# Filling transfers moved from SyncE's queue to GpSimd's, with new planner constants, in a four-layer attention kernel

## The chip, the core and the metric

The kernel runs on one core of a Trainium2 chip. The time is the device time of one execution in microseconds (us). Engines are named as in the profile: PE (TensorE), ACT (ScalarE), DVE (VectorE), POOL (GpSimd) and SP (SyncE, which only issues DMAs here).

## What is computed

Four layers with residuals: attention A, linear attention B, then A and B again with the same weights. S is 2048, D is 512, and there are 32 heads of 16. In A all heads share one K and V.

```python
def _A_ref(x, wq, wk, wv, wo):
    q = (x @ wq).reshape(B, S, H, Dh).transpose(0, 2, 1, 3)
    k = x @ wk
    v = x @ wv
    scores = jnp.einsum("bhqd,bkd->bhqk", q, k) * (Dh ** -0.5)
    p = _softmax(scores, axis=-1)
    o = jnp.einsum("bhqk,bkd->bhqd", p, v)
    return o.transpose(0, 2, 1, 3).reshape(B, S, H * Dh) @ wo
...
x = x + _A_ref(_layernorm(x), A_wq, A_wk, A_wv, A_wo)
x = x + _B_ref(_layernorm(x), B_wqkv, B_wo)      # phi(q) (phi(k)^T v) / den, then @ wo
x = x + _A_ref(_layernorm(x), A_wq, A_wk, A_wv, A_wo)
x = x + _B_ref(_layernorm(x), B_wqkv, B_wo)
```

## The kernel before

**A planner writes the order.** The kernel is a program that records operations (`op`, with the engine, a duration, what is read and written, and a priority) and plays them through in a model of the engines (`Planner`, L36). Whatever is ready first by the model, and of these the lowest priority number, is next on its engine. The order that comes out is fixed at build time. On the chip every engine goes through its list strictly in order, and waits on semaphores where data or a buffer is not there yet. So durations in the code are plan times: they decide the order, not how long something takes.

**Attention layers (L = 0 and 2, `run_a`, L950).** The 2048 scores blocks of a layer (128 keys by 512 columns, 16 query tiles x 2 parities x 16 key tiles x 4 row groups) are made on PE by L959, three to four row groups at a time. The exponential of a block is taken in one of two ways:

- ACT takes two or three blocks at once (L1139) into a PT buffer, and PE multiplies them with V into the accumulator bank (L1013).
- DVE makes an approximate exponential of one block (L1225): it adds a constant to the scaled scores and reads the int16 bits as a bf16 number. Four blocks make a chunk in an FB buffer of 128x2048. The approximation is smoothed with three more copies of the chunk, each with another constant added to the int16 bits, and weighted copies of V (`VW`). So each DVE block costs PE four multiplications.

A copy is made in one of two ways. DVE makes it with one instruction for the chunk (L1273). Or two DMAs make one of the three: a **filling transfer** (`prime`, L1285, issued at L1297) first writes the constant from a row in DRAM (`shift_row`) into a free FB buffer, and an **addition** (`dma_shift`, L1304, issued at L1306) then adds the finished chunk to that buffer in the DMA engines. Up to NPRE = 2 buffers stand filled ahead (`primed`). `dve_shifts` (L1253) takes the DMA way for a chunk when a filled buffer is there, more than DMIN query segments are left, and the planned end of the DMA backlog (`pl.dmaq`) is less than DQ ahead.

**Queues.** Fillings are issued from SP (hardware queue q1 of the profile), additions from POOL (software queue q0). SP also issues the DMA transposes (`dmat`, L737): 24 of `OT<-Osb` in the epilogues of the attention layers (`epilogue`, L1396), which the product with `wo` on PE (L731) reads, and 36 of `xnT<-xn` (12 at the start, 24 for the tiles of the B layers that are worked on beside the attention). POOL also does two small operations of each layer norm (L813, L815), on which DVE waits at L818. SP and POOL, too, wait in order: a filling at the head of its queue that waits for PE to finish with its buffer holds all that stands behind it.

**Plan times of the DMAs.** An operation with `xfer=(a, b)` is planned to land at `dmaq + b`, where `dmaq` is moved on by `a` after the issue's own duration and `lat` (L191 to L193): one line for fillings and additions together. A filling has 0.54 + 0.2 for the issue and (DPF, DTAIL), an addition has PGEN + 0.3 = 0.95 + 0.3 and (DXF, DTAIL). A transpose has 0.1 and DTL = 4.0, outside of `dmaq`.

**Constants by stage.** The module's constants (L368 to L441) hold until `act_stream` replaces some of them: at L1066 the first attention layer applies `TUNE[0]` at the very start, and at L1069 each attention layer applies its own dictionary. Nothing is reset, so what TUNE[0] sets and TUNE[2] doesn't also holds in layer 2. The other thresholds: CHT, CHE, ENDL (how many blocks ahead DVE may take from), FBO, FBS, FBP (how many FB buffers must stay free for a new chunk, for copies, for a filling), AHEAD, BLS, BLT, BLO, DXB (how much planned work DVE may have in front of it when it is given a block), STICK (whether PE keeps its mode), LAG (how long an engine waits for a more urgent operation).

**B layers (`run_b`, L1461)** have little PE and ACT work, much of it laid beside the attention layers. The change touches nothing there.

Of the kernel before, what the change touches and what calls it, by code (L numbers as in the profile page):

```python
# [8 lines left out]
I16 = mybir.dt.int16  # L9
# [3 lines left out]
PE, AC, DV, PO, SP = "pe", "act", "dve", "pool", "sp"  # L13
ENGS = (PE, AC, DV, PO, SP)

P = 128
# [19 lines left out]
class Planner:  # L36
# [41 lines left out]
    def op(self, opts, reads=(), writes=(), prio=5.0, lat=0.08, dma=False, name="", join=None, mode="full", port=False, after=(), behind=(), xfer=None):  # L78

        o = Op()  # L80
        o.opts, o.prio, o.users, o.done, o.end = opts, prio, [], False, None
        o.eng, o.fn, o.n, o.value, o.sem, o.signal, o.isdma = None, None, None, None, None, False, dma
        o.name = (name, lat)
        o.freed = False
        o.begun = None
        o.cols = 0
        o.mode = mode
        o.port = port
        o.xfer = xfer
        deps = set()  # L90
        for k in reads:
            deps.update(self.ws(k))
        for k in list(writes) + list(after) + list(behind):
            deps.update(self.ws(k))
            deps.update(self.readers.get(k, ()))
        if join is not None:
            deps.update(join.deps)
            deps.discard(join)
        for k in writes:
            if join is not None and join in self.ws(k):  # L100
                self.writer[k] = self.ws(k) + [o]
            else:
                self.writer[k] = [o]
                self.readers[k] = []
        for k in list(reads) + list(after):
            if k not in writes:
                self.readers.setdefault(k, []).append(o)
        o.deps = deps
        o.left = 0
        chain = len(opts) == 1 and PE in opts  # L110
        for d in deps:
            if not (d.done or (chain and d.freed and d.eng == PE)):
                o.left += 1
                d.users.append(o)
        if o.left == 0:
            self._eligible(o)
        return o
# [226 lines left out]
class Seg:  # L344
# [11 lines left out]
    def take(self, js, back=False):  # L356
# [22 lines left out]
LAG = 0.15  # L379
# [16 lines left out]
BLS = 1.4  # L396
BLO = 5.0
DXB = 2.0
BLT = 2.5
# [18 lines left out]
CHB = 4  # L418
FBO = 2
FBS = 4  # L420
AHEAD = 20
CHT = 19
PSH = False
STICK = 1.5
# [4 lines left out]
DMIN = 4  # L429
NPRE = 2  # L430
EVEN = True
CHE = 8
AVOID = True
PGEN = 0.95
DPF = 2.2
DXF = 2.8
DTAIL = 1.6
DQ = 4.0
FBP = 4
TUNE = {0: {"DXF": 4.5, "DTAIL": 2.0, "CHT": 26, "FBO": 1, "FBS": 3, "AHEAD": 8, "BLS": 2.3, "BLT": 2.8, "FBP": 4, "DQ": 6.0, "DMIN": 4, "LAG": 0.25, "BLO": 3.5, "STICK": 2.5, "DXB": 2.0},  # L440
        2: {"CHE": 8, "DMIN": 3, "NPRE": 2, "BLS": 1.7}}  # L441


def bass_interleave_layers__grouped_kv_mqa__linear_attn_block__prompt_kernel(
# [12 lines left out]
    op = pl.op  # L457
# [39 lines left out]
    FB = sb("FB", [P, NFB, CHB * 512], BF16)  # L497
# [23 lines left out]
    pts, fbs = {}, {}  # L521
# [28 lines left out]
    def once(tag, keys):  # L550
        if tag in seen:
            return ()
        seen.add(tag)
        return keys

    def guest(L, kind, i, h=None):
        return once((L, kind, i, h), home[kind, i]) if (kind, i) in home else ()
# [131 lines left out]
    cst = nc.dram_tensor("shift_row", (1, CHB * 512), I16, kind="Internal").ap()  # L689

    def fb_keys(i):
        return [("FB", i, h) for h in range(CHB)]
# [46 lines left out]
    def until(*keys):  # L739
        for k in keys:  # L740
            yield ("ops", pl.ws(k))
# [208 lines left out]
    def run_a(L):  # L950
# [23 lines left out]
        def spend(h, o):  # L974
            h[0] -= 1
            if o not in h[1]:
                h[1].append(o)
            if h[0] == 0:
                pl.give_after(h[2], h[3], h[1])
# [85 lines left out]
        def act_stream():  # L1065
            if L == 0:  # L1066
                globals().update(TUNE[0])
            yield ("flag", ("K", L, 0))
            globals().update(TUNE[L])  # L1069
            if L:  # L1070
# [214 lines left out]
        def prime():  # L1285
            yield ("flag", ("K", L, T - 1))
            if L == 0:
                row = FB[0:1, NFB - 1, :].bitcast(I16)
                op({DV: (0.6, lambda e: e.memset(row, DSH * 128 // NSH))}, writes=fb_keys(NFB - 1), prio=1.0)
                op({SP: (0.54, lambda e: e.dma_start(cst, row))}, reads=fb_keys(NFB - 1), writes=["cst"], prio=1.0, lat=2.5, dma=True)  # L1290
            yield from until("cst")
            while state["si"] < len(segs) - DMIN:
                if len(primed) >= NPRE or len(fb_pool.free) <= FBP or fb_pool.wait:
                    yield ("sleep", 0.2)
                    continue
                g_ = yield ("acq", fb_pool, 9.0)
                o = op({SP: (0.54, lambda e, g_=g_: e.dma_start(fbs[g_].bitcast(I16), cst.to_broadcast([P, CHB * 512])))}, reads=["cst"], writes=fb_keys(g_), prio=9.0,  # L1297
                       lat=0.2, dma=True, behind=guest(L, "FB", g_), xfer=(DPF, DTAIL))
                primed.append((g_, o))
            while primed:  # L1300
                g_, o = primed.pop()
                pl.give_after(fb_pool, g_, [o])

        def dma_shift(blk, f_, hold, g_, o):  # L1304
            pl.stat["dma"] += 1
            o = op({PO: (PGEN, lambda e: e.dma_start(fbs[g_].bitcast(I16), fbs[f_].bitcast(I16), accum_op=ALU.add))}, reads=fb_keys(f_), writes=fb_keys(g_), prio=0.0, lat=0.3,  # L1306
                   dma=True, xfer=(DXF, DTAIL))
            spend(hold, o)
# [32 lines left out]

        pl.process(spare())
        pl.process(prime())
        for i in pairs:
            pl.process(spare_sacc(i))
# [564 lines left out]
```

## Time and profile before

| | |
|---|---|
| median of 3 runs | 1512.31 us (1508.14 to 1513.63) |
| the profiled execution | 1501.68 us |
| its span, first to last instruction | 1499.9 us |
| attention layers, steady parts | 10 to 620 us and 850 to 1410 us |
| B layers alone | about 700 to 850 us, and from 1410 us |
| additions (L1306) | 163, on POOL |
| fillings (L1297) | 167, on SP |

The profile gives for each group of instructions the busy time, the mean duration of one, and the idle time of the engine before them with what ended it. "Us to landing" of a DMA is from the start of its issuing instruction to the last step of its semaphore. A wait is put down to the semaphore that came last. SP is shown as SPq since it is never busy, and a DMA's own time shows only in the shares of the queues.

### The profile page before, as it was taken

Reading aid. Unit: us, or ns where it says so; the run is one execution under the profiler, and the core shown is the slowest. Engines: PE = TensorE matmul, PEld = TensorE weight load, DVE = VectorE, ACT = ScalarE, POOL = GpSimd, SP = SyncE. Lnnn points to the kernel's source line nnn. Section 1 sums busy time; section 2 is a strip of 40 time slices with the busy share of each in tenths; the row PEclk is TensorE's granted clock in tenths of the full one; section 3 lists DMA queues with packets and bytes.
Section 4 is the critical chain, followed back from the end, with each engine's and each line's share of the span. In section 5 each row is a group of like instructions: output and inputs, shape, how many; then the busy total and the mean of one; then the engine's idle time right before and its main releaser. Section 6 shows DMA issues by size and latency. Waiting matters only on the chain.

```text
span 1499.9 us, 37236 instructions
## 1 busy us (share of the span) xinstructions
PE 1403.9 (94%) x14791; PEld 509.3 (34%) x14906; DVE 1416.7 (94%) x2615; ACT 1444.2 (96%) x1511; POOL 245.8 (16%) x353
## 2 busy tenths in 40 slices
PE   7999999999989899999999999998999999999998
PEld 4333333233323233233644332332333333333335
DVE  7999999999989999999876999998999999999996
ACT  8999999999989999999799999998999999999996
POOL 5111121111111112000111111121211111111001
PEclk9999999999999999999999999999999999999999
DMA  4766767666676667311000276766767666766101
GB/s 118 208 150 148 181 144 180 168 148 158 150 159 155 150 154 174 85 29 51 9 2 2 58 173 144 161 150 148 164 161 170 170 156 147 173 158 161 24 16 57
DMA packets 89021, 191.72 MB, mean 128 GB/s; under 512 B 39441, under 2 KB 46097, under 8 KB 88850
## 3 DMA queue, kind: packets, MB, share of 16 engines
q0 software_dynamic: 23472, 85.47, 30.5%
q1 hardware_dynamic: 65378, 103.87, 23.3%
q8 instruction: 120, 1.97, 0.5%
q14 instruction: 51, 0.42, 0.1%
HBM read 93.88 MB, written 2.10 MB: 64 GB/s over the span
## 4 chain that ended last, share of the span: by engine, by line
PE 20%; ACT 15%; DVE 13%; issue 5%; DMA 3%; POOL 1%; ACTq 0%; POOLq 0%
ACT PT L1139 9%; PE ps L1013 6%; PE ps L959 6%; ACT xnT L1139 4%; DVE FB L1225 4%; PE ps L731 3%; DVE FB L1273 3%; PE ps L1058 2%; PE ps L892 1%; DMA FB<-FB 1%; DVE OBB L1225 1%; DVE sacc L1225 1%; DMA OBB<-FB 1%; DMA xn<-FB 1%; ACT phE L1467 1%
## 5 line engine op out<-in xcount | busy, mean ns | idle before, releaser
L1139 ACT ACTIVATE PT<-ps 128x1024 bf16<-128x1024 f32 (+1 forms) x946 | 1005.8, 1169 | 12.9 <-PE ps L959 11.4
L959 PE MATMUL ps<-QT,KM 32*128 32x512 bf16 x4096 | 537.5, 385 | 44.1 <-ACT PT L1139 19.0
L1225 DVE TENSOR_SCALAR FB<-ps 128x512 int16<-128x512 f32 x828 | 545.7, 683 | 18.2 <-PE ps L959 16.8
L1013 PE MATMUL ps<-FB,VW 128*32 128x512 bf16 x3247 | 452.5, 385 | 7.3 <-DVE sacc L1359 1.7
L1013 PE MATMUL ps<-PT,V 128*32 128x512 bf16 x2097 | 380.9, 388 | 13.8 <-ACT PT L1139 5.5
L959 PEld LDWEIGHTS ps<-QT,KM 32*128 32x128 bf16 x4096 | 134.6, 91 | 425.3 <-ACT PT L1139 194.2
L1139 ACT ACTIVATE xnT<-ps 128x1024 bf16<-128x1024 f32 (+1 forms) x238 | 261.9, 1152 | 7.2 <-PE ps L959 6.9
L1273 DVE TENSOR_SCALAR FB<-FB 128x2048 int16<-128x2048 int16 x365 | 244.9, 681 | 0.2
L1139 ACT ACTIVATE OBB<-ps 128x1024 bf16<-128x1024 f32 (+1 forms) x166 | 182.2, 1144 | 3.2 <-PE ps L959 3.2
L1013 PEld LDWEIGHTS ps<-FB,VW 128*32 128x32 bf16 x3247 | 109.9, 94 | 128.2 <-issue 75.8
L1058 PE MATMUL ps<-QT,V 128*32 128x512 bf16 (+6 forms) x623 | 150.3, 318 | 1.3 <-DVE FB L1225 0.7
L1306 POOL DMA_DIRECT2D FB<-FB x77 | 77.0, 1001 | 426.1 <-DVE FB L1225 314.3
L1013 PEld LDWEIGHTS ps<-PT,V 128*32 128x32 bf16 x2097 | 91.9, 93 | 100.6 <-issue 48.2
L1013 PE MATMUL ps<-xnT,V 128*32 128x512 bf16 x524 | 121.2, 388 | 1.3 <-ACT xnT L1139 0.6
L1013 PE MATMUL ps<-OBB,V 128*32 128x512 bf16 x361 | 83.5, 390 | 2.7 <-ACT PT L1139 1.4
L813 POOL TENSOR_SCALAR ve<-mv 128x1 f32<-128x1 f32 x64 | 30.7, 482 | 316.2 <-DVE mv L812 314.7
L1058 PEld LDWEIGHTS ps<-QT,V 128*32 128x32 bf16 x623 | 48.5, 95 | 69.0 <-issue 47.1
L731 PE MATMUL ps<-wqkv,xnT 128*128 128x512 bf16 (+1 forms) x204 | 64.9, 370 | 3.9 <-issue 2.1
L1013 PE MATMUL ps<-wq,VW 128*32 128x512 bf16 x256 | 63.2, 386 | 0.3 <-issue 0.3
L1013 PE MATMUL ps<-xn,VW 128*32 128x512 bf16 x275 | 62.8, 384 | 0.1
L1013 PE MATMUL ps<-OBB,VW 128*32 128x512 bf16 x237 | 57.7, 388 | 1.2 <-DVE sacc L1359 0.8
L1225 DVE TENSOR_SCALAR xn<-ps 128x512 int16<-128x512 f32 x81 | 53.7, 683 | 1.2 <-PE ps L959 1.0
(210 smaller groups left out, 1650.7 us busy)
## 6 DMA issues: line engine op xcount, KB each, us to landing
FB<-shift_row SPq DMA_DIRECT2D x115, 512.0 KB, 4.8
FB<-FB POOLq DMA_DIRECT2D x77, 512.0 KB, 5.7
sacc<-shift_row SPq DMA_DIRECT2D x15, 512.0 KB, 4.5
wo<-shift_row SPq DMA_DIRECT2D x15, 512.0 KB, 5.7
sacc<-FB POOLq DMA_DIRECT2D x12, 512.0 KB, 5.1
FB<-xn POOLq DMA_DIRECT2D x12, 512.0 KB, 5.4
wo<-FB POOLq DMA_DIRECT2D x11, 512.0 KB, 5.4
OBB<-shift_row SPq DMA_DIRECT2D x10, 512.0 KB, 6.2
```

What stands on the lines that cost most here:

```text
L731: return e.matmul(dst, lhsT=l, rhs=r, start=(k == 0), stop=(k == len(pairs) - 1))
L813: op({PO: (0.1, lambda e: e.tensor_scalar(out=ve[:, t:t + 1], in0=mv[:, t, 1:2], scalar1=1e-5, scalar2=None, op0=ALU.add))}, reads=[("mv", ...
L892: ins = e.matmul(dst[:, g * P:(g + 1) * P], lhsT=lhs(g, k), rhs=rhs(k), start=(k == 0), stop=(k == FT - 1))
L959: return e.matmul(bank(b), lhsT=KM[r, sg.par, kt * P:(kt + 1) * P], rhs=QT[r, sg.t, :], start=True, stop=True)
L1013: ins = e.matmul(ps[32 * j:32 * j + 32, ACC * 512:(ACC + 1) * 512], lhsT=V[:, kt, :] if w is None else VW[:, kt, w, :], rhs=ap, start=(k = ...
L1058: o = op({PE: (n / 2400.0, lambda e: e.matmul(ps[32 * j:32 * j + 32, b * 512:b * 512 + n], lhsT=V0[:], rhs=QT[:, sg.t, 0:n], start=st, sto ...
L1139: ex = op({AC: (0.051 + 0.4267 * n, lambda e, n=n, s_=s_, p_=p_: e.activation(pts[p_][:, 0:n * 512], ps[:, s_ * 512:(s_ + n) * 512], ACTF. ...
L1225: o = op({DV: (0.602, lambda e: e.tensor_scalar(out=dst.bitcast(I16), in0=bank(b), scalar1=VB, scalar2=VLO, op0=ALU.add, op1=ALU.max))}, w ...
L1273: o = op({en: (du, lambda e, w=w, g_=g_: e.tensor_scalar(out=fbs[g_][:, 0:n].bitcast(I16), in0=fbs[f_][:, 0:n].bitcast(I16), scalar1=float ...
L1306: o = op({PO: (PGEN, lambda e: e.dma_start(fbs[g_].bitcast(I16), fbs[f_].bitcast(I16), accum_op=ALU.add))}, reads=fb_keys(f_), writes=fb_k ...
L1467: op({AC: (0.07 + n / 1200.0, lambda e: e.activation(phE[:, i, 0:n], bank(b, n), ACTF.Exp))}, reads=[B_(b)], writes=[("phE", i)], prio=pr ...
```

## The change

Three things change. The filling is issued by POOL instead of SP, with the plan time of an addition's issue (PGEN = 0.95) and 0.3 after it. The module's DPF, DXF and DTAIL are 2.0, 3.4 and 2.0. And both TUNE dictionaries are new; TUNE[0] no longer sets DXF, DTAIL, FBO, AHEAD, BLT, DQ or STICK.

```diff
 PGEN = 0.95
-DPF = 2.2
-DXF = 2.8
-DTAIL = 1.6
+DPF = 2.0
+DXF = 3.4
+DTAIL = 2.0
 DQ = 4.0
 FBP = 4
-TUNE = {0: {"DXF": 4.5, "DTAIL": 2.0, "CHT": 26, "FBO": 1, "FBS": 3, "AHEAD": 8, "BLS": 2.3, "BLT": 2.8, "FBP": 4, "DQ": 6.0, "DMIN": 4, "LAG": 0.25, "BLO": 3.5, "STICK": 2.5, "DXB": 2.0},
-        2: {"CHE": 8, "DMIN": 3, "NPRE": 2, "BLS": 1.7}}
+TUNE = {0: {"CHT": 26, "FBS": 3, "BLS": 1.2, "BLO": 5.0, "DXB": 0.8, "FBP": 3, "DMIN": 3, "LAG": 0.25},
+        2: {"FBO": 3, "FBP": 6, "DQ": 6.0, "NPRE": 2, "LAG": 0.2, "BLS": 1.7, "BLO": 7.0, "CHT": 26, "DMIN": 2}}
...
-                o = op({SP: (0.54, lambda e, g_=g_: e.dma_start(fbs[g_].bitcast(I16), cst.to_broadcast([P, CHB * 512])))}, reads=["cst"], writes=fb_keys(g_), prio=9.0,
-                       lat=0.2, dma=True, behind=guest(L, "FB", g_), xfer=(DPF, DTAIL))
+                o = op({PO: (PGEN, lambda e, g_=g_: e.dma_start(fbs[g_].bitcast(I16), cst.to_broadcast([P, CHB * 512])))}, reads=["cst"], writes=fb_keys(g_), prio=9.0,
+                       lat=0.3, dma=True, behind=guest(L, "FB", g_), xfer=(DPF, DTAIL))
```

Since the order is planned, it changes on every engine. The built program of the changed kernel has 193 additions and 197 fillings, all of them on POOL, and on SP only loads, transposes and stores are left.

## The prediction

> **What bounds the kernel now.** I read the page's first part, then the busy time of five stretches: the two attention layers (their steady parts, 10 to 620 us and 850 to 1410 us), and three windows of 50 us in them with lost time (columns after the length: PE, weight loads, DVE, ACT, POOL; clock; DMA share).
>
> ```profile
> span 1499.9 us, 37236 instructions
> PE 1403.9 (94%) x14791; PEld 509.3 (34%) x14906; DVE 1416.7 (94%) x2615; ACT 1444.2 (96%) x1511; POOL 245.8 (16%) x353
> 10.00:620.00 610.00, 574.17 (x6014) 191.90 (x6059) 593.83 (x1076) 599.65 (x612) 112.94 (x148) 0.99 0.67 158
> 850.00:1410.00 560.00, 525.33 (x5579) 176.44 (x5615) 548.89 (x986) 548.85 (x563) 94.32 (x106) 0.99 0.66 152
> 400.00:450.00 50.00, 43.58 (x444) 13.82 (x446) 44.18 (x78) 44.16 (x45) 7.11 (x9) 0.93 0.65 140
> 500.00:550.00 50.00, 45.16 (x493) 14.70 (x494) 47.87 (x86) 47.63 (x50) 8.72 (x10) 1.00 0.69 154
> 1000.00:1050.00 50.00, 44.68 (x478) 16.12 (x481) 44.41 (x81) 44.57 (x48) 8.46 (x8) 0.93 0.59 137
> ```
>
> In the attention layers ACT is busy for 599.65 of 610 and 548.85 of 560 us, with DVE as full beside it. ACT bounds the kernel, and only 10.35 + 11.15 = 21.5 us of its idle time there can be won. Of that, 5.84 + 2.37 + 5.43 us lie in the three windows. What ended the waits in them (first row: 417 to 425 us, then 498 to 512, 1208 to 1222, 1004 to 1020; us in total, times, longest), and who waited for the DMA transposes of L737 in the whole span:
>
> ```profile
> ACT OBB L1139 <- PE ps L959: 3.0, 1, 3.0
> ...
> ACT PT L1139 <- PE ps L959: 2.3, 1, 2.3
> ...
> ACT PT L1139 <- PE ps L959: 1.2, 1, 1.2
> ...
> ACT xnT L1139 <- PE ps L959: 4.6, 2, 4.0
> PE ps L1013 <- DMA FB<-FB: 3.6, 1, 3.6
> ...
>   PE ps L959: 5.8, 2
> ...
>   PE ps L731: 2.2, 1
> DMA to landing us min/median/max: 2.4/2.7/8.9
> ```
>
> The lost time has two sources. One addition (L1306) held PE for 3.6 us and ACT for 4.6. Three late transposes held PE for 5.8 + 2.2 = 8.0 us, and ACT for 3.0 + 2.3 + 1.2 = 6.5. The change can act through these two kinds of lateness, or through the work itself.
>
> **The change, part by part.** *What is really planned.* The diff raises the module's DXF from 2.8 to 3.4, but that value was not in force: TUNE[0] was applied from the first instant (L1066) and never taken back, so every addition of before was planned with DXF 4.5, DTAIL 2.0. The new TUNE has neither, so an addition's plan goes from 0.95 + 0.3 + 4.5 + 2.0 = 7.75 us to 0.95 + 0.3 + 3.4 + 2.0 = 6.65: shorter, not longer. A fill's goes from 0.54 + 0.2 + 2.2 + 2.0 = 4.94 to 5.25. A transpose keeps 0.1 + 4.0. What they took (last column, us to landing):
>
> ```profile
> FB<-shift_row SPq DMA_DIRECT2D x115, 512.0 KB, 4.8
> FB<-FB POOLq DMA_DIRECT2D x77, 512.0 KB, 5.7
> ```
>
> The median addition (5.7) still lies inside 6.65 and the median fill inside 5.25.
>
> *Work.* Counted in the built order, DVE blocks (L1225) go from 1114 to 1116, shift copies on DVE (L1273) from 665 to 644 whole ones and from 15 to 0 short ones, additions from 163 to 193, fills from 167 on SP to 197 on POOL. ACT's exponentials (L1139) go from 1068 of 1024 columns and 282 of 1536 to 1100 and 260; ACT also loses six copies (3 va, 3 xnT) and gains three.
>
> ```profile
> L1273 DVE TENSOR_SCALAR FB<-FB 128x2048 int16<-128x2048 int16 x365 | 244.9, 681 | 0.2
> L1139 ACT ACTIVATE PT<-ps 128x1024 bf16<-128x1024 f32 x741 | 744.9, 1076 | 11.7 <-PE ps L959 10.3 <-PE ps L1013 0.4
> L1139 ACT ACTIVATE PT<-ps 128x1536 bf16<-128x1536 f32 x205 | 303.5, 1505 | 1.2 <-PE ps L959 1.1
> ```
>
> DVE: 21 x 244.9/365 = 14.1 us less, the 15 short ones between 0 and 15 x 0.67 = 10 (I take 5), two blocks more at about the same 0.67: -18 us. ACT: 32 x 744.9/741 - 22 x 303.5/205 = -0.4 us; three copies of 512 columns, each no more than the 1.0 us of 1024: **-2 us** in all, the range -0.4 to -3.4. So DVE is relieved but ACT, which bounds, is not: the 18 us are cover, not time.
>
> *Issue on POOL.* Each of the 197 fills now costs POOL an issue like an addition's:
>
> ```profile
> L1306 POOL DMA_DIRECT2D FB<-FB x77: 852/871/2431, 48.2 to 1384.9; - x77
> SPq L1297 <- PE ps L1013: 192.9, 72, 12.8
> DVE xn L818 <- POOL rs L815: 10.8, 18, 1.2
> ```
>
> With 30 more additions that is 227 x 0.87 to 227 x 2.43, or 200 to 550 us, on an engine busy for 245.8 of 1499.9: hidden. What queues behind a fill counts more: on SP fills waited for PE to free their buffer (72 times for L1013 alone), and on POOL the next addition and the layer norm's L813 and L815 stand behind that wait. DVE waits 10.8 us for L815 now; twice that is the price if it grows with the issues, and the 18 us above cover it. I take 0, with 0 to +10 as the range.
>
> The Trainium skill, page "DMA: Bandwidth & Descriptors", section "SWDGE vs HWDGE vs iDMA", speaks against this part: GpSimd writes its descriptors into SBUF, from which DVE's two-port modes lock it out, while DMAs issued from SP are immune. The median of 871 ns beside a minimum of 852 shows little of that here; at the maximum for every fill the sum would still stay on POOL.
>
> *Additions.* One late addition cost ACT 4.6 us. The chain's longest DMA pieces, and the two queues in 1006.5 to 1010 us, while the first of them was under way:
>
> ```profile
> 959.30 9.01 DMA xn<-FB
> 1005.68 11.40 DMA FB<-FB
> 1098.92 9.09 DMA OBB<-FB
> ...
> 1006.58 0.32 SPq L1297 DMA_DIRECT2D sacc<-shift_row  x1
> 1007.44 0.32 SPq L1297 DMA_DIRECT2D OBB<-shift_row  x1
> 1008.53 0.32 SPq L1297 DMA_DIRECT2D FB<-shift_row  x1
> ...
> q1 hardware_dynamic: 142, 0.54, 64.2%
> ```
>
> Fills issued after the addition overtook it on the other queue: in that window only q1 moved. In one queue, behind it, they can't. I take **-5 us**; the range goes to +15, if 193 additions planned 1.1 us shorter come late one time in twenty, by 1.5 us each.
>
> *Transposes.* They now have SP's queue to themselves, but everything else shares q0. The two queues while an addition (issued just before, landing at 507.8) and the transpose of 501.67 were both under way, 503 to 505.5 us, and once the addition had drained, 506 to 507.5 (packets, MB, share of 16 engines); then the whole run:
>
> ```profile
> q0 software_dynamic: 134, 0.48, 101.6%
> q1 hardware_dynamic: 76, 0.02, 5.9%
> OT<-Osb SPq DMA_TRANSPOSE x1, 6.6
> ...
> q1 hardware_dynamic: 398, 0.14, 58.1%
> q0 software_dynamic: 20, 0.02, 16.2%
> ...
> 501.67 1.45 SPq L737 DMA_TRANSPOSE OT<-Osb  x1
> 503.23 1.11 SPq L1297 DMA_DIRECT2D wq<-shift_row  x1
> ...
> q0 software_dynamic: 23472, 85.47, 30.5%
> q1 hardware_dynamic: 65378, 103.87, 23.3%
> ```
>
> While q0 has packets the transpose gets 76 small ones in 2.5 us, against 398 in 1.5 us afterwards: it advances by small packets between large ones and in effect lands when q0 runs dry (6.6 us; planned 4.1). Two fills issued after it (the first at 503.23) did not hold it, for they stood behind it in its own queue. After the change they would be in q0 and pass it. Load of q0 over the 1170 us of the two stretches: before, 0.305 x 1499.9 = 457 us of all engines (2.81 an addition), 39%. After, 193 x 2.81 = 542 and 197 fills at no more than 0.233 x 1499.9 / 167 = 2.09 us, 412: 954 us, 81%.
>
> The Trainium skill, same page, section "Queues, rings and completion order", says that each engine round-robins between queue rows a packet at a time, a packet being typically 9 to 17 descriptors. The turns agree with the rows; the size doesn't, for 76 transpose records against 134 of q0 is less than one to a turn. By the page's size a transpose would need few turns, and the rival "faster" below would hold.
>
> Price: if lateness grows with q0's share (39 to 81%), the 8.0 us of PE waits become 17; if with share over free share (0.64 to 4.3), 54. Between ends so far apart I take 28, near the 17, because the plan lets an addition start only under a bounded backlog: 20 us more on PE. ACT lost 6.5 for 8.0, but the 400 us window lost 5.84 for one stall of 3.0, since the clock fell to 0.93; I count one for one: **+20 us**, range -6.5 (all transposes on time) to +46.
>
> *Sum:* 20 - 5 - 2 + 0 = +13 us. The profiled execution took 1501.68 us, its span 1499.9 and 1.8 around it; with the change 1514.7. It lies 10.6 us below the median of the three runs shown (1512.31), and I take the same distance afterwards: **1525 us**, +0.9%.
>
> **The rivals.**
> *Faster.* One queue in order makes landings regular, and a transpose is hardly held. Place: L737 and L1306. For it: the three additions of 9 to 11 us and the overtaking. Against it: 76 against 398 packets. It decides if transposes still land within 4.1 us under q0's load. Price -6.5 - 5 - 2 = -13.5: 1512.31 - 13.5 = **1499**, and down to 1491 with all 21.5 us won.
> *No change.* q0's backlog stays short, since fills are issued when buffers come free and not at random; transposes lose only what additions win, +7: **1512**.
> *Slower still.* The 1.1 us taken from the plan of additions, and fills holding POOL's queue while they wait for PE, make additions late too: 46 + 15 + 10 - 2 = +69 at the far end of all, half of it more likely: **1545**.
> *It doesn't do what it says.* The longer plan is none, as shown; that is already in the sum.
>
> **How the numbers follow.** Forecast 0.38, slower still 0.14, no change 0.26, faster 0.22. A difference within 0.5% (7.6 us) is about what a measurement of this kernel can't tell from none. Forecast and "slower still" both give slower: 0.52; same 0.26; faster 0.22. The range leaves out a tenth on either side: the lower half of "faster" (below 1497) and the upper half of "slower still" (above 1550). The forecast's own range is 1515 to 1538.
>
> **What would show it.** Right: PE waits for `OT<-Osb` and `xnT<-xn` grow from 8.0 us to 20 or more and the transposes' median landing rises above 4 us; more windows with a clock under 1.00; the chain has fewer additions over 8 us; ACT's busy time stays within 3 us of 1444, DVE's falls by about 18. Wrong: transposes land at 2.7 as before, or PE waits mostly for additions, or ACT's busy time moves by over 5 us, which would mean that the plan and not the queues decides.

## The result and the profile after

The changed kernel takes 1549.94 us (median of 4 runs, 1543.25 to 1554.53), the kernel before, run beside it, 1512.97 (4 runs, 1508.14 to 1514.02). The ratio is **1.0247, 95% interval 1.0204 to 1.0291**: slower by 37 us. The forecast was 1525, +0.9%. The profiled execution of after took 1550.07 us.

The page of after, its first part, then queues, then DMA issues (last column: us to landing):

```profile
span 1548.3 us, 37399 instructions
...
PE 1423.3 (92%) x14803; PEld 510.5 (33%) x14915; DVE 1410.5 (91%) x2584; ACT 1447.5 (93%) x1518; POOL 394.9 (26%) x580
...
q0 software_dynamic: 56160, 204.50, 58.4%
q1 hardware_dynamic: 41330, 16.30, 5.4%
...
FB<-shift_row POOLq DMA_DIRECT2D x142, 512.0 KB, 7.0
FB<-FB POOLq DMA_DIRECT2D x91, 512.0 KB, 5.7
```

ACT does almost the same work (1444.2 us before, 1447.5 now), but its idle time rose from 1499.9 - 1444.2 = 55.7 to 1548.3 - 1447.5 = 100.8 us. So the span's 48.4 us are 45.1 of idle ACT and 3.3 of work. The additions land as before (5.7), but a filling now needs 7.0 us instead of 4.8. Who waited for the transposes of L737 in the kernel after:

```profile
  PE ps L731: 21.2, 7
  PE ps L959: 11.9, 4
...
  PE ps L892: 9.8, 3
...
DMA to landing us min/median/max: 2.4/4.8/13.7
```

PE lost 21.2 + 11.9 + 9.8 = **42.9 us** to late transposes, against 8.0 before. The median landing went from 2.7 to 4.8 us, past the planned 4.1, and the longest to 13.7. For the additions of L1306 in the kernel after, the same view has:

```profile
  PE ps L1013: 1.9, 3
...
DMA to landing us min/median/max: 4.5/5.7/12.9
```

In the kernel before it has:

```profile
  PE ps L1013: 6.5, 6
```

So the additions did win something, and the transposes lost far more. In the chain of waits of after the longest DMA pieces (start, us) are now mostly transposes, where before three additions stood:

```profile
1009.24 12.85 DMA OT<-Osb
...
1127.03 10.37 DMA xnT<-xn
1158.25 13.69 DMA OT<-Osb
...
1277.06 10.62 DMA FB<-wo
1362.35 9.78 DMA xnT<-xn
1461.41 9.00 DMA OBB<-FB
```

One of them from close by, in the timeline of after (start, us, engine; in brackets the idle time before and what ended it):

```profile
1123.18 1.16 POOL L1306 DMA_DIRECT2D FB<-FB  x1 [3.90 <-DVE FB L1225]
...
1124.29 1.20 POOL L1297 DMA_DIRECT2D wq<-shift_row  x1
...
1125.58 2.63 POOL L1297 DMA_DIRECT2D FB<-shift_row  x3
1127.03 1.20 SPq L737 DMA_TRANSPOSE xnT<-xn  x1
1131.13 0.90 POOL L1306 DMA_DIRECT2D wq<-wo  x1 [2.92 <-DMA wq<-shift_row]
1133.07 0.87 POOL L1306 DMA_DIRECT2D FB<-FB  x1 [1.04 <-DMA FB<-shift_row]
...
1137.44 0.61 PE L892 MATMUL ps<-xnT,wqkv 128*128 128x128 bf16 x4 [5.98 <-DMA xnT<-xn]
```

POOL waited for DVE and then issued an addition and four fillings in a burst. The transpose of 1127.03 met them, two more additions were issued while it was under way, and it landed after 10.37 us. PE, in its fixed order, stood for 5.98 us. What that cost (windows of after; ACT's busy time is the fourth pair, the clock the third number from the end):

```profile
10.00:640.00 630.00, 575.76 (x6005) 191.86 (x6050) 589.92 (x1061) 599.05 (x606) 174.61 (x246) 0.98 0.73 162
870.00:1460.00 590.00, 541.93 (x5597) 176.94 (x5630) 548.04 (x973) 552.92 (x577) 172.86 (x222) 0.96 0.82 180
...
1125.00:1131.00 6.00, 5.77 (x76) 1.61 (x68) 6.00 (x11) 6.00 (x8) 3.22 (x5) 1.00 0.91 263
1131.00:1137.00 6.00, 0.39 (x3) 0.10 (x3) 2.00 (x4) 1.86 (x3) 1.77 (x2) 0.72 1.04 213
1137.00:1143.00 6.00, 5.56 (x39) 2.24 (x39) 2.44 (x4) 3.03 (x4) 0.00 (x0) 0.50 0.78 154
1143.00:1149.00 6.00, 6.00 (x39) 1.94 (x34) 4.68 (x9) 4.15 (x5) 0.00 (x0) 0.64 0.01 3
1149.00:1155.00 6.00, 5.84 (x62) 1.81 (x59) 5.70 (x12) 6.00 (x7) 1.50 (x2) 1.00 0.71 154
```

ACT lost 4.14 + 2.97 + 1.85 = 9.0 us for a PE wait of 6.0. PE was busy again from 1137.44 on, but at half clock, and it didn't feed ACT fast enough until about 1147. In the attention layers (first two rows) ACT is now idle for 30.95 + 37.08 = 68 of 1220 us, where it was 21.5 of 1170.

### The profile page after: what moved, and what is told of

Its sections match the earlier page's. It is cut to its first block, busy times and chain, and to the rows that moved or that the text cites. A ratio compares the mean times of both kernels' runs of the same rounds, so it can differ in the third digit from the quotient of the medians.

```text
span 1548.3 us, 37399 instructions
## 1 busy us (share of the span) xinstructions
PE 1423.3 (92%) x14803; PEld 510.5 (33%) x14915; DVE 1410.5 (91%) x2584; ACT 1447.5 (93%) x1518; POOL 394.9 (26%) x580
## 5 line engine op out<-in xcount | busy, mean ns | idle before, releaser
L959 PE MATMUL ps<-QT,KM 32*128 32x512 bf16 x4096 | 544.2, 391 | 49.6 <-ACT PT L1139 15.2
L1225 DVE TENSOR_SCALAR FB<-ps 128x512 int16<-128x512 f32 x780 | 515.1, 679 | 55.1 <-PE ps L959 53.7
L1013 PE MATMUL ps<-FB,VW 128*32 128x512 bf16 x3224 | 431.9, 387 | 7.5 <-DVE sacc L1359 2.4
L1273 DVE TENSOR_SCALAR FB<-FB 128x2048 int16<-128x2048 int16 x328 | 221.3, 682 | 0.6
L1139 ACT ACTIVATE OBB<-ps 128x1024 bf16<-128x1024 f32 (+1 forms) x167 | 186.5, 1147 | 10.7 <-PE ps L959 10.6
L1306 POOL DMA_DIRECT2D FB<-FB x91 | 87.6, 962 | 337.9 <-DVE FB L1225 227.2
L1297 POOL DMA_DIRECT2D FB<-shift_row x142 | 120.8, 889 | 50.4 <-PE ps L1013 41.5
L1013 PE MATMUL ps<-xnT,V 128*32 128x512 bf16 x510 | 112.4, 394 | 2.1 <-ACT PT L1139 1.3
L1225 DVE TENSOR_SCALAR sacc<-ps 128x512 int16<-128x512 f32 x88 | 58.3, 681 | 7.9 <-PE ps L959 7.6
L1013 PE MATMUL ps<-xn,VW 128*32 128x512 bf16 x264 | 57.0, 386 | 0.6 <-DVE sacc L1359 0.4
L731 PE MATMUL ps<-wo,OT 128*128 128x512 bf16 x91 | 33.5, 420 | 25.5 <-DMA OT<-Osb 21.2
```

What stands on the lines that cost most here:

```text
L731: return e.matmul(dst, lhsT=l, rhs=r, start=(k == 0), stop=(k == len(pairs) - 1))
L959: return e.matmul(bank(b), lhsT=KM[r, sg.par, kt * P:(kt + 1) * P], rhs=QT[r, sg.t, :], start=True, stop=True)
L1013: ins = e.matmul(ps[32 * j:32 * j + 32, ACC * 512:(ACC + 1) * 512], lhsT=V[:, kt, :] if w is None else VW[:, kt, w, :], rhs=ap, start=(k = ...
L1139: ex = op({AC: (0.051 + 0.4267 * n, lambda e, n=n, s_=s_, p_=p_: e.activation(pts[p_][:, 0:n * 512], ps[:, s_ * 512:(s_ + n) * 512], ACTF. ...
L1225: o = op({DV: (0.602, lambda e: e.tensor_scalar(out=dst.bitcast(I16), in0=bank(b), scalar1=VB, scalar2=VLO, op0=ALU.add, op1=ALU.max))}, w ...
L1273: o = op({en: (du, lambda e, w=w, g_=g_: e.tensor_scalar(out=fbs[g_][:, 0:n].bitcast(I16), in0=fbs[f_][:, 0:n].bitcast(I16), scalar1=float ...
```

## The experiments

**Theory.** The fillings in q0 make the transposes land later than the plan says, PE waits, its clock falls, ACT starves. **Rivals:** the new plan itself (constants, order, 30 more additions) costs the time; or POOL, held by fillings that wait for buffers, delays additions and layer norms. Each ratio below is to the kernel before, run beside that experiment; its median was 1507 to 1508 us there.

### The same plan with the fillings on SP, and the old plan with them on POOL

In both kernels every engine keeps its planned order, and only the issue of the fillings changes sides, after the planning. First the kernel after with all 197 on SP:

```diff
+            o.eng, o.fn, o.t = e, fn, self.now
...
+    fills = [o for o in pl.order[PO] if o.name[0] == "fill"]; [setattr(o, "eng", SP) for o in fills]; pl.order[PO] = [o for o in pl.order[PO] if o not in fills]; pl.order[SP] = sorted(pl.order[SP] + fills, key=lambda o: o.t); pl.finalize()
```

> The changed kernel with its plan kept (the same order on PE, DVE and ACT, instruction for instruction), but its 197 fillings are issued from SP, in the order of their planned start. Theory (the fillings in the additions' queue starve the transposes): PE's waits for transposes fall from 42.9 us to about 10, the time from 1550 us to 1510 to 1520. Rival A (the new plan itself, with additions planned 1.1 us shorter and new thresholds, is what costs): the time stays above 1540. Rival B (fillings that wait for PE hold POOL's queue): the time falls too, but the transposes' waits stay at 35 us or more.

Measured: 1501.42 us, ratio to before 0.9966 (0.9948 to 0.9985), faster than the 1510 to 1520 expected. Its waits for transposes (L737), then for additions (L1306):

```profile
  PE ps L892: 0.6, 1
...
DMA to landing us min/median/max: 2.4/2.5/7.3
```

```profile
  PE ps L1013: 13.5, 11
```

Then the kernel before with its 167 fillings on POOL (the same edit with PO and SP exchanged):

> The kernel before with its plan kept (the same order on PE, DVE and ACT), but its 167 fillings are issued from POOL, in the order of their planned start. Theory: PE's waits for transposes rise from 8.0 us to 30 or more, the median landing of a transpose from 2.7 to 4 us or more, and the time from 1513 to 1535 to 1550. Rival A (the new plan): the time stays within 1505 to 1520.

Measured: 1529.32 us, ratio 1.0162 (1.0139 to 1.0186), a little less than expected. Its waits for transposes:

```profile
  PE ps L731: 28.3, 7
...
DMA to landing us min/median/max: 2.4/3.9/13.0
```

So the queue alone costs 1.0247 / 0.9966 = 1.028 on the new plan and 1.016 on the old one, and the new plan alone wins 0.3%. The rival "the plan costs it" falls. The gain that the single queue brings for additions is real too (13.5 to 1.9 us on the new plan, 6.5 to 0.8 on the old), and it is the smaller part.

### Half of the fillings on SP

```diff
+    fills = [o for o in pl.order[PO] if o.name[0] == "fill"][::2]; [setattr(o, "eng", SP) for o in fills]; pl.order[PO] = [o for o in pl.order[PO] if o not in fills]; pl.order[SP] = sorted(pl.order[SP] + fills, key=lambda o: o.t); pl.finalize()
```

> The changed kernel with its plan kept and every second filling issued from SP (99 on SP, 98 on POOL). Theory: PE's waits for transposes grow faster than q0's load: with a load between the two ends they are 8 to 18 us (0.6 with all fillings on SP, 42.9 with none), and the time is 1508 to 1520, nearer to the 1501 of the one end than to the 1550 of the other. Rival (proportional): 20 to 24 us and 1522 to 1530.

Measured: 1506.96 us, ratio 0.9992 (0.9971 to 1.0014); PE waited 12.8 us for transposes and 3.5 for additions, with q0 at 47.2%. The theory had this, but for a time a little below its range. So half of the traffic brings much less than half of the loss.

### Planning the transposes later

If lateness beyond the plan is the cause, a plan that expects it must remove the loss with all fillings left on POOL. The plan time of the 48 transposes of the attention layers is changed, first to 10 us, later to 7:

```diff
-        return op({SP: (0.1, lambda e: e.dma_start(dst, src, transpose=True))}, reads=reads, writes=writes, prio=prio, lat=DTL, dma=True, behind=after)
+        return op({SP: (0.1, lambda e: e.dma_start(dst, src, transpose=True))}, reads=reads, writes=writes, prio=prio, lat=DTL if ("K", 0, T - 1) not in pl.flags else 10.0, dma=True, behind=after)
```

> The changed kernel with transposes planned at 10.0 us instead of 4.0 once the first layer's K is complete; nothing else is edited, but the planner makes a new order from it (ACT gets 21 more blocks, some 9 us). Theory: PE's waits for transposes fall from 42.9 us to below 10, which is worth some 35 us, less the 9 us: 1520 to 1530. Rival A (the plan of the additions and the thresholds): no less than 1545. Rival B (POOL's queue is held): no less than 1545, with POOL's waits as they were.

Measured: 1511.76 us, ratio 1.004 (1.0001 to 1.0078), faster than expected. PE waited 0.5 us for transposes, which landed after 2.4/5.7/19.0 us, and 9.8 for additions; ACT's busy time was 1456.6, 9 us more, since this plan gave it more blocks. That speaks against POOL as the cause: it issued almost as much (195 fillings and 191 additions).

> The changed kernel with transposes planned at 7.0 us instead of 4.0 once the first layer's K is complete; a new order, with the work on ACT and DVE within 3 us of the changed kernel's. Theory: PE's waits for transposes fall from 42.9 us to 8 to 15 (a quarter of the transposes land later than 8 us), the time from 1550 to 1512 to 1525. Rival (what costs is not the transposes' lateness): 1540 or more.

Measured: 1505.55 us, ratio 0.9985 (0.9962 to 1.0009), faster than the 1512 to 1525 expected. Its waits for transposes, of which 8 to 15 us were expected to stay:

```profile
  PE ps L731: 0.8, 1
...
DMA to landing us min/median/max: 2.4/4.8/11.9
```

The transposes land about as late as in the kernel after (median 4.8), and almost nothing waits for them. **One number in the plan, with the order that follows from it, gives back the whole loss.** The time that was lost was not the transfers' own, but that of an order that didn't know of them.

Does the kernel before lose time in the same way, with its 8.0 us? (The same edit there, with 7 us.)

> The kernel before with transposes planned at 7.0 us instead of 4.0 once the first layer's K is complete. Theory: the 8.0 us of PE waits for transposes go to 2 or less, which is worth 5 to 8 us; the work on ACT hardly changes: 1503 to 1509. Rival (transposes are not what the plan of before lacks): 1510 to 1518.

Measured: 1504.12 us, ratio 0.9995 (0.9977 to 1.0012). The time lies in the expected range, but the kernel before was about as fast beside it, so this is a miss: PE no longer waits for transposes at all, and the 5 to 8 us (0.3 to 0.5%) don't come of it. I had counted these waits as winnable time.

### What of it is the transposing

The 48 transposes are plain copies of the same bytes; the transposition is left out.

```diff
-        return op({SP: (0.1, lambda e: e.dma_start(dst, src, transpose=True))}, reads=reads, writes=writes, prio=prio, lat=DTL, dma=True, behind=after)
+        return op({SP: (0.1, (lambda e: e.dma_start(dst, src, transpose=True)) if ("K", 0, T - 1) not in pl.flags else lambda e: e.dma_start(dst, src.rearrange("p (g c) -> p g c", c=P)))}, reads=reads, writes=writes, prio=prio, lat=DTL, dma=True, behind=after)
```

> The changed kernel with all 48 DMA transposes after the first layer's K issued as plain copies of the same 128 KB (the transposition is left out, so what is computed from them is meaningless); the order on every engine is kept. A copy for OT has 128 packets of 1 KB, 8 to an engine; one for xnT has pieces of 256 B, 32 to an engine, as a transpose. Theory (a packet of SP's queue gets a turn only after a packet of q0, so what counts is the number of packets): the waits of PE for OT fall from 33 us to 10 or less, those for xnT stay at 10 to 20, and the time is 1515 to 1530. Rival A (any transfer of SP's queue is held until q0 is empty): waits above 35 us, time above 1540. Rival B (it is the transposing itself that conflicts with q0): both on time, waits below 8 us, 1500 to 1512.

Measured: 1502.65 us, ratio 0.9975 (0.9950 to 1.0000). Waits for L737:

```profile
  PE ps L731: 8.0, 5
...
  PE ps L892: 5.7, 2
...
DMA to landing us min/median/max: 2.0/4.5/10.3
```

No side had all of this: the time is that of rival B, but of 42.9 us of waits 13.7 are left, where it had less than 8. The median hardly falls (4.8 to 4.5), the longest landing does (13.7 to 10.3). A plain copy comes late beside this traffic too, by 6 us at most against the planned 4.1; a transpose comes late by nearly 10.

### The constants by themselves

The new constants, with the fillings planned and issued on SP as before:

```diff
-                o = op({PO: (PGEN, lambda e, g_=g_: e.dma_start(fbs[g_].bitcast(I16), cst.to_broadcast([P, CHB * 512])))}, reads=["cst"], writes=fb_keys(g_), prio=9.0,
-                       lat=0.3, dma=True, behind=guest(L, "FB", g_), xfer=(DPF, DTAIL))
+                o = op({SP: (0.54, lambda e, g_=g_: e.dma_start(fbs[g_].bitcast(I16), cst.to_broadcast([P, CHB * 512])))}, reads=["cst"], writes=fb_keys(g_), prio=9.0,
+                       lat=0.2, dma=True, behind=guest(L, "FB", g_), xfer=(DPF, DTAIL))
```

> The new constants alone: fillings planned and issued on SP with 0.54 and 0.2 as before, all else as changed; the planner makes a new order (196 additions, 200 fillings, the work on ACT and DVE as in the changed kernel to a few us). Theory (the queue costs, the constants don't): 1497 to 1510, PE's waits for transposes 10 us or less. Rival (the constants cost): 1520 or more.

Measured: 1530.25 us, ratio 1.0147 (1.0083 to 1.0211): the rival was right. PE waits for additions in this kernel:

```profile
  PE ps L1013: 22.5, 15
```

The same with DXF back at the value that was in force before:

```diff
-DXF = 3.4
+DXF = 4.5
```

> The new constants with fillings planned and issued on SP, as in the run of the constants alone, but additions planned with DXF 4.5 as they were in force before (168 additions and 172 fillings instead of 196 and 200; ACT has some 9 blocks more). Theory (with two queues an addition needs the longer plan: 1.1 us less costs late additions): PE's waits for additions fall from 22.5 us to 10 or less, the time from 1530 to 1503 to 1515. Rival (the other thresholds cost): 1522 or more.

Measured: 1504.34 us, ratio 0.9982 (0.9968 to 0.9995), and

```profile
  PE ps L1013: 4.7, 3
```

So in this pair the plan that is shorter by 1.1 us, and the 28 additions more that come with it, cost 1.6% with fillings on another queue. The size of that isn't general: the kernel after with its fillings moved to SP has the shorter plan too, with 13.5 us of waits for additions, and took 0.9966. Why 22.5 us cost so much more than 13.5 was not found out. In one queue PE waits 1.9 us, so there is little left there for a longer plan to win; that was not run. Alone, the new constants cost 1.5% and the queue 1.6%; together they cost 2.5%. Neither part could be judged alone.

The kernel after planned with DXF 4.5 (as in the last diff) and its fillings then moved to SP (as in the first):

> As the run with the changed plan and all fillings issued from SP (1501 us), but additions planned with DXF 4.5, from which the planner makes a new order (160 additions; 20 more blocks on ACT, some 9 us). Theory: PE's waits for additions fall from 13.5 us to 5 or less, which the 9 us on ACT eat up: 1500 to 1512. Rival (additions' lateness costs nothing there): 1508 to 1516.

Measured: **1499.93 us, ratio 0.995 (0.993 to 0.9969)**, the lowest ratio of all. Against 0.9966 without the longer plan the intervals overlap: PE's waits for additions fell from 13.5 to 4.0 us, and ACT's busy time rose from 1443.0 to 1451.4.

### How a transpose is held

No attention is computed in the next three kernels; transposes of the same size are issued beside set numbers of fillings (f) and additions (a) of the same size, four times each.

> No attention is computed: 15 cases, four trials of each, of one 128 KB transpose issued from SP at the moment at which POOL begins to issue 0, 1, 2, 4 or 6 fillings or 1, 2, 4 additions, or with fillings on SP behind or ahead of it, and a plain copy with 1 KB packets in three of the cases; the output is the input x. Theory (32 packets to an engine, one to a turn, with q0's packets of 0.2 to 0.35 us between): alone 2.4 us; 5 to 6 with 2 fillings, 9 to 10 with 4 fillings and no more with 6 (32 turns are over); 4.5, 7 and 12 with 1, 2 and 4 additions; 2.4 with fillings on SP behind it; 5 to 6 with two of them ahead; a plain copy (8 turns) 4 to 5 with 4 fillings or additions. Rival (held until q0 is empty): a plain copy is as late as the transpose, and 6 fillings hold longer than 4.

Measured: alone 2.4 us; with 1, 2, 4, 6 f 3.6, 4.1, 3.9, 3.7; with 1, 2, 4 a 3.1, 3.2, 3.2. A miss, and by its design: POOL began 0.46 us after SP, so the transpose was well under way before q0 had anything. Hence a kernel in which SP waits until POOL has issued all:

> No attention is computed, the output is the input x: as the 15 cases before, but SP issues its transfer only after POOL has issued all of its own, so that it finds q0 moving. Fillings took about 1.1 us each there and additions 2.1. Theory (a turn for each of 32 packets): a transpose lands in some 3 us behind 1 filling, 5 behind 4, 8 behind 8, 4, 7 and 11 behind 2, 4 and 6 additions, that is with the drain of q0, while a plain copy (8 turns) takes 4 at most. Rival (any transfer is held until q0 is empty): the plain copy is as late as the transpose. Second rival (q0 doesn't hold SP's queue much): neither over 4.5.

Its view of DMA issues (us to landing; behind 4 and 8 f in q0, behind 6 a, behind 4 f in SP's own queue, and a plain copy behind 8 f):

```profile
to_pfd<-x SPq DMA_TRANSPOSE x4, 7.4
...
to_pfh<-x SPq DMA_TRANSPOSE x4, 12.1
...
to_paf<-x SPq DMA_TRANSPOSE x4, 13.4
...
to_sad<-x SPq DMA_TRANSPOSE x4, 8.0
...
to_cfh<-x SPq DMA_DIRECT2D x4, 128.0 KB, 7.7
```

The transpose lands when q0 is empty: behind 1 to 8 f it takes 3.9 to 12.1 us, 1.2 more for each; behind 1 to 6 a 4.4 to 13.4, 1.8 more for each. The theory had the order of these but not the size (5 us behind 4 f, 8 behind 8), and its 4 us at most for a plain copy were 7.7 to 8.2. But 4 f ahead in its *own* queue cost just as much (8.0). Then why does the same traffic hold transposes in the kernel after, and not in the one with the fillings on SP? The last kernel issues the transpose behind one or two a, and more f behind *it* (`a`, `f` and `be` are the numbers of a case; `go` is what SP waits for):

```python
# POOL
for i in range(a):
    e.dma_start(bufs[4 + i][:].bitcast(I16), src[:].bitcast(I16), accum_op=ALU.add).then_inc(po_, 16)
e.memset(tick[:], 0.0).then_inc(go, 1)
for i in range(f):
    e.dma_start(bufs[6 + i][:].bitcast(I16), row.to_broadcast([P, 2048])).then_inc(po_, 16)
# SP
e.wait_ge(go, g)
...
    e.dma_start(dst[name][:], x[:, 0, :], transpose=True).then_inc(sp_, 16)
for _ in range(be):
    e.dma_start(bufs[k][:].bitcast(I16), row.to_broadcast([P, 2048])).then_inc(sp_, 16)
    k += 1
```

> No attention is computed here and the output is the input x; the total time means nothing, only the landing of the transposes from the view of DMA issues. Each group of transposes is issued from SP once one or two additions stand in GpSimd's queue q0; then 0, 2, 4 or 6 fillings are issued right behind it, in q0, or 4 on SP's own queue. My theory, that fillings issued after a transpose still pass it in q0, because the two queues are served by turns, while those behind it in SP's own queue cannot: behind two additions alone a transpose lands after 6.3 us as before, with 2, 4 and 6 fillings issued behind it in q0 after about 8.5, 10.7 and 12 to 13 us, and with 4 behind it on SP's queue after 6.3; behind one addition 4.4 alone, 8 to 9 with 4 fillings behind it in q0, 4.4 with 4 on SP. The rival, that what counts is only what had been issued before the transpose: 6.3 in every group with two additions and 4.4 in every group with one, wherever the fillings behind go. In the second case the longer landings of the changed kernel must come from fillings issued ahead of the transposes alone.

In the same view: behind 2 a alone, then with 2, 4 and 6 f issued behind it in q0, and 4 behind it on SP; then behind 1 a alone, with 4 f behind it in q0, and on SP:

```profile
to_ahead<-x SPq DMA_TRANSPOSE x4, 6.3
to_pbb<-x SPq DMA_TRANSPOSE x4, 10.0
to_pbd<-x SPq DMA_TRANSPOSE x4, 12.4
to_pbf<-x SPq DMA_TRANSPOSE x4, 12.6
to_sbd<-x SPq DMA_TRANSPOSE x4, 7.0
to_one<-x SPq DMA_TRANSPOSE x4, 4.4
to_opd<-x SPq DMA_TRANSPOSE x4, 9.1
to_osd<-x SPq DMA_TRANSPOSE x4, 4.5
```

The rival (only what was issued first counts) falls. **Fillings issued after a transpose pass it if they are in q0, and wait behind it if they are in its own queue**: 9.1 against 4.5 us. There is an end to that: the fifth and sixth filling behind it cost only 0.2 us more. A plain copy behind 2 a is passed too, but by less: it lands after 5.7 us alone, 8.3 with 4 f behind it in q0, and 6.8 with them on SP.

In the kernel after both sources are there. Counted by issue and landing in its trace, a transpose of the attention layers found 1.43 fillings and 0.89 additions under way, and 1.02 and 0.93 were issued before it landed. In the same order with fillings on SP it found 0.27 and 0.81, and the 1.85 fillings issued after it, before it landed, stood behind it.

## Why the prediction was right and wrong, point by point

**What bounds the kernel: right.** ACT bounds it, its work hardly moved, and the time went into late DMAs for which PE stood.

**The plan times: right.** The "longer" DXF is a shorter one. What follows from it depends on the queue: 1.9 us of waits in one queue, 13.5 in two with the same order, and 22.5 with the order that is planned for two, where DXF 4.5 leaves 4.7.

**Work: about right for the instructions, not for the busy time.** ACT's busy time was to fall by 2 us and rose by 3.3; DVE's fell by 6.2 (1416.7 to 1410.5), not 18. But instructions overlap in the profile, and busy time counts an overlap once. The durations of all instructions, added up, fell by 3.2 us on ACT and by 25.6 on DVE. The kernel with the same instructions and the fillings on SP was busy for 1443.0 us on ACT, 4.5 less than the kernel after: with stalls between them, instructions overlap less.

**Issue on POOL: right.** POOL's busy time rose to 394.9 us and cost nothing that shows; DVE's wait for L815 went from 10.8 to 9.2 us. The kernels with transposes planned at 7 and 10 us issue as much and don't lose the time.

**Additions, -5: right, as far as PE's waits for them show.** They went from 6.5 to 1.9. The example of an overtaken addition, at 1005.68 in the kernel before, was read too simply: its issue on POOL took 2.43 us, against a median of 0.87, so part of its lateness came before any filling passed it.

**Transposes, +20: the step that failed.** The mechanism was the right one, and the term was far too small, for two reasons.

- *PE waits:* 28 us were taken, between 17 and 54 and "near the 17, because the plan lets an addition start only under a bounded backlog". It was 42.9. That bound is on additions, and the burst of four fillings above shows that it doesn't hold the backlog that a transpose meets. Traffic behind the transpose counts as well, as the last kernel shows.
- *ACT's loss for a us of PE wait:* one for one was taken, though the prediction had seen one stall of 3.0 us cost 5.84. Waits for transposes and additions together rose by 34.9 - 4.6 = 30.3 us, and ACT's idle time by 45.1: 1.5 for one, like the 9.0 for 6.0 of the stall shown above. In the windows above the excess lies where the clock is at 0.50 to 0.64. The mean clock of the whole span went from 0.995 to 0.976: at half rate that is about 2 x 0.024 x 1548.3 = 74 us of lower clock, against 15 before. That the lower clock makes up all of the excess was not shown.

The Trainium skill, page "TensorE: Matmul & The Clock Gate", section "What's actually happening", has the clock at half rate after at least one window of about 3.4 us without work, and back at full rate after at least one such window of it. The half rate agrees with the 0.50 above. The times are not those of one window: PE's last work ended at 1131.46, and a mean of 0.72 over 1131 to 1137 puts the fall at about 1133.6, 2.2 us later. PE worked again from 1137.44, and a mean of 0.64 over 1143 to 1149 puts the return at about 1147, ten us later.

**The sum.** For the profiled execution it was 20 - 5 - 2 = +13, and it came to 48.4: about 50 - 5 + 3.3. The last step, the distance of 10.6 us from the profiled execution to the median, hid part of that miss: the kernel after was profiled right at its median (1550.07 and 1549.94).

**Turns.** The prediction cited the Trainium skill, page "DMA: Bandwidth & Descriptors", section "Queues, rings and completion order": an engine serves its queues by turns, a packet each. The last kernel agrees with turns, since what comes later in the other queue passes, and passes only up to an end. My reading was that with packets of the size that the Trainium skill gives a transpose would need few turns, and so would hardly be held. It landed after up to 13.4 us, against 2.4 alone. Whether its turns are more than that or q0's are long can't be read from these runs.

**The rivals.** "Faster" fell for the reason given against it. "Slower still" (1545) had nearly the time, but by a mechanism that wasn't there: additions weren't late. Fillings did wait on POOL for PE (52.6 us, 26 times), but neither PE's waits for additions (1.9 us) nor DVE's for L815 (9.2) grew. "No change" is what the same change gives with the transposes planned at 7 us (0.9985).

**What would show it.** Waits of 20 us or more (42.9), a median landing above 4 us (4.8), more time at a low clock, two additions of 9 us or more in the chain instead of three: all there. ACT within 3 us of 1444 was just missed (3.3).

## What to carry to other kernels

When a transfer changes its queue, look first at what else shares the DMA engines and has a planned landing: its plan time has to move too, as it did from 4.1 to 7.1 us here, where that was worth 2.6%. Where a planner writes the order, move the issue after the planning as well, with the order kept; that separates what the queue costs (2.8% here) from what the order costs (-0.3%). And price a stall of PE not at its length but by a stall in the trace of before, with what the clock does after it. Take that as an upper price: the 8.0 us in the kernel before were worth nothing that shows.

## What the hardware showed that I had not expected

- A transpose that starts 0.46 us before q0's traffic is held only 0.7 to 1.7 us, whether one transfer follows or six (3.1 to 4.1 us against 2.4). One that starts behind a queue of them lands with its drain.
- A plain copy of the same size is held differently: about 8 us behind 4 or 8 fillings and behind 4 or 6 additions alike, where the transpose went from 7.4 to 12.1 us and from 9.9 to 13.4. Why was not found out.
- 8.0 us of PE waits for transposes in the kernel before were worth nothing measurable (0.9995 without them, in another order), while 30 us more of waits for transposes and additions came with 45 us more of idle ACT. What makes up for the small ones was not found out.
